# Attention and mixture-of-experts in one kernel: the attention's steps in a new order, token reads on half the array's rows, small work moved between engines

## The chip, the cores and the metric

The kernel runs on one core of a Trainium2 chip. The metric is the device time of one execution in microseconds (us). Before the change the median of 3 runs is 542.32 us (542.18 to 542.85).

## The reference

Two parts follow each other: an attention between tokens and a few states, and a mixture of experts over all their results.

```python
B, H, S, Ns, D = (8, 8, 512, 32, 64)
scores = scale * x @ state^T                 # (B, H, 512, 32)
a = softmax(scores)                          # over the 32 states
xread = a @ state                            # token reads, (B, H, 512, 64)
scores2 = scale * state @ x^T                # (B, H, 32, 512)
a2 = softmax(scores2)                        # over the 512 tokens
sread = a2 @ x                               # state reads, (B, H, 32, 64)
x = concat(xread, sread) -> (B, 544, 512)    # heads side by side
logits = x @ w_gate                          # 8 experts
local_gate = sigmoid(x @ w_local)
for b, s:                                    # in order of s
    e = argmax(logits[b, s]) if s == 0 or local_gate[b, s] < 0.5 else e of s - 1
    p = softmax(logits[b, s])
    out[b, s] = p[e] * (relu(x[b, s] @ w1[e]) @ w2[e])
```

The 8 expert layers are 512 to 1024 to 512 wide, and 8 x 544 = 4352 rows go through them. All data are float32.

## The kernel before

The kernel has three stages: attention, routing, experts. The scheduler is off: every engine executes its instructions in the order in which the program issues them.

**Attention** takes the batches one by one. The 8 heads of a batch are two groups u = 0 and 1 of four heads k; one PSUM tile s of 128 x 512 holds for one u the scores of 4 heads x 32 states against 512 tokens. The class Attention has one small method for each step, and the string STEPS gives the order: each word is a two-letter code and its indices, batch first, then the group u or a 128-token chunk c. So `tr20` is the turn of batch 2, group 0. What each step is, with its engine and its line of the profile:

| codes | engine, line | what it does |
|---|---|---|
| xt, xn | SP, L273, L277 | loads halves of a batch's transposed tokens x_t (512 KB each), its tokens x_n (1 MB) |
| sc | PE, L307 | scores, 16 matmuls on 64x32 tiles of the array |
| mx, nb | DVE L315, POOL L319 | maxima over tokens; times -scale |
| et, iv | ACT L323, DVE L328 and L329 | exponents over tokens with their sums; 1 over the sum |
| tu, ec | PE L377, ACT L381 | these exponents transposed; the copy to SBUF |
| sr, st, ws | PE L390, ACT L396, SP L405 | state reads; scaled; to DRAM |
| rt, sl, sk | DVE L400, PE L410, DVE L414 | state reads turned; the states' logits; their copy into lt |
| tr, mo, sb | DVE L334, DVE L337, POOL L344 | scores turned in 32x32 blocks; maxima over states; subtracted |
| ex, zh, zs, zi, ml, tb | ACT L348, POOL L355, DVE L358, DVE L363, POOL L367, DVE L371 | exponents; half sums; sums; reciprocals; products, called shares; turned back, as a |
| lg, lt | PE L422, DVE L426 | token logits from a; turned into the tile lt |
| vv, xr, wr | PE L432, ACT L438, SP L446 | token reads of a chunk; their copy to SBUF; to the DRAM tensor rows |
| ga, gl, sd | PE L289, ACT L294, ACT L268 | states times gate weights; kept as gl; states put into the blocks of a block-diagonal tile sd |
| ch, kp, wm, go | | choice of experts for batches 0 to 6; filler matmuls; hand over to the routing |

Token logits need no token reads: a times (states times gates) gives them. So the reads vv may come late, and about a third of them stand behind the first `go`. Two PSUM pools of four banks each serve the stage: sp for the scores, p for all other results of PE.

**Routing** (Routing.route) first makes the choice for batch 7 (`self.choose(lt, B - 1, B)`: six small DVE instructions on lt), then turns `top`, scans it along the tokens, turns it back, counts tokens by expert with two matmuls (`tot`, `pre`), and by some forty small DVE instructions finds each token's slot. At seven places it calls `reads()`, which issues the steps up to the next `go`. ACT has a few instructions in this chain: the exponent `pr` (L553), `less` (L607), `behind` (L612). Then matmuls of 0/1 matrices (L710) give the tokens of each slot, and GpSimd gathers the first rows (L827).

**Experts**: up to 24 pairs of 128-row blocks. The first pair is plain matmuls (L1100), the later ones use a seven-product scheme (L1016, L1056), with weights loaded by SP (L873) and sums on DVE (L930).

Of the kernel before, what the change touches and what calls it, by code (L numbers as in the profile page):

```python
# [8 lines left out]
F32 = mybir.dt.float32  # L9
# [3 lines left out]
Alu = mybir.AluOpType  # L13
AX = mybir.AxisListType.X
# [4 lines left out]
P = 128  # L19
B, H, S, N, DH = 8, 8, 512, 32, 64  # L20
D = H * DH
E, F = 8, 1024
T = S + N
# [127 lines left out]
sc0 kp3 xt11 xt10 mx00 ga kp2 sd3 tr01 xt21 mx01 sd2 mo01 nb0 tr00 et01 sb01 xn0 mo00 wm14 sc1 et00 sb00 ex01  # L151
iv0 tu01 tr11 gl tu00 zh01 ex00 tr10 xt20 ec00 zh00 zs01 mo10 sd0 xn1 zs00 sb10 zi0 ec01 mx11 sd1 sr0 ml01 mo11
ex10 mx10 sc2 ml00 st0 xt30 tb01 rt0 sb11 tb00 sl0 xt31 tr20 lg0 nb1 ex11 zh10 sk0 tr21 vv03 et10 zh11 xt41 zs10
vv00 et11 lt0 mx21 xr03 xt51 zs11 tu11 zi1 xr00 tu10 iv1 ml11 mo21 vv02 xt50 ec10 mo20 ml10 sc3 ec11 tb11 xt40
xr02 mx20 sb21 sr1 tb10 xn2 tr30 sb20 ex21 lg1 mx30 st1 vv12 zh21 ex20 rt1 tr31 nb2 sl1 zh20 et20 vv10 zs21 sk1
lt1 ws1 zs20 et21 tu20 zi2 xt60 mo30 xr10 ml20 sc4 xr12 iv2 mx31 ec20 xn3 ml21 tu21 tb20 vv11 mx41 ec21 nb3 sb30
et30 tb21 sr2 tr40 et31 xt61 lg2 mo31 ex30 tu30 mo40 sb31 st2 sc5 lt2 wr00 xr11 mx40 ec30 zh30 tr41 wr03 tu31
ex31 nb4 zs30 sb40 vv23 et40 mx50 xt70 ec31 mo41 tu40 zh31 ex40 rt2 sr3 sb41 zs31 ws0 xr23 zi3 xn5 et41 iv3 sl2
ml31 mx51 vv22 ex41 sk2 iv4 st3 ml30 tb31 sc6 xr22 rt3 ec40 zh41 tb30 xt71 sl3 zh40 zs41 lg3 tr50 nb5 vv31 wr02
zs40 et50 zi4 vv01 xn4 lt3 xr31 ml40 mo50 sk3 tr51 xr01 vv13 ml41 tb40 et51 vv21 mo51 sb50 xr13 wr10 iv5 vv20  # L160
tb41 xr21 sb51 xn6 mx60 ex50 lg4 mx61 xr20 zh50 tu50 ex51 lt4 tu41 tr60 nb6 ec50 zh51 tu51 zs50 et60 mo60 vv32
wr20 ec51 zs51 sb60 zi5 tu60 ec41 wr23 tr61 sc7 xr32 ml50 wr11 ex60 mo61 sr4 et61 ml51 tb50 wr12 mx71 sr5 sb61
ws2 st4 tb51 ec60 ws3 vv30 tr70 zh60 ex61 xn7 mx70 st5 lg5 zh61 xr30 zs60 tu61 mo70 nb7 et70 vv40 zs61 sb70 zi6
ec61 tu70 lt5 wr22 iv6 xr40 ml61 rt5 sr6 rt4 ex70 tr71 wr40 ec70 ml60 mo71 sl5 et71 wr13 sl4 sk5 tb61 vv41 sb71
st6 wr31 tb60 tu71 zh70 ex71 sk4 iv7 wr32 lg6 rt6 xr41 zs70 zh71 sl6 ec71 lt6 wr21 vv42 zs71 zi7 wr01 sr7 sk6
xr42 ml71 ch0 wr42 vv33 st7 ml70 wr41 vv50 tb71 xr33 wr33 tb70 vv53 xr50 rt7 wr30 lg7 xr53 sl7 lt7 wr53 vv51 sk7
go wr50 vv43 xr51 wr51 go xr43 vv52 wr43 vv61 xr52 ws4 vv60 wr52 xr61 go ws5 xr60 vv62 wr60 go xr62 ws7 wr62
vv71 wr61 vv72 xr71 wr71 vv63 xr72 wr72 vv70 xr63 go wr63 go xr70 wr70 ws6 go vv73 xr73 wr73
# [3 lines left out]
class Attention:  # L172


    def __init__(self, ctx, tc, p, late, xn, xt, st, stt, wgl, wgs, lt, rows, none):
# [14 lines left out]
        self.sttc = [once.tile([P, n, KT, N], F32, name=f"sttc{i}") for i, n in enumerate((1, B - 1))]  # L190
# [3 lines left out]
        self.states_of = once.tile([P, B * G * DH], F32, name="states_of")  # L194
        nc.sync.dma_start(out=self.states_of, in_=st)
        nc.sync.dma_start(out=self.sttc[1], in_=stt[:, 1:])
        nc.sync.dma_start(out=wgs.rearrange("p w k e -> p (w k e)"), in_=wgl)
# [3 lines left out]
        self.sd = late.tile([P, B, G * GD], F32, name="sd", bufs=1)  # L201
# [10 lines left out]
    def clear(self):  # L212
        nc = self.nc
        for z in self.zh:
            nc.vector.memset(z[:, :, N // 2:], 1e-9)
        for z in self.z2:
            nc.vector.memset(z[:, :, 1:], 1e-9)
        nc.gpsimd.memset(self.gl, 0.0)
        nc.gpsimd.memset(self.lt, 0.0)
        nc.gpsimd.memset(self.sd, 0.0)  # L220
        nc.gpsimd.memset(self.none, 0.0)
# [8 lines left out]
    def reads(self):  # L230
# [4 lines left out]
                  ec=self.turned_to, iv=self.invert, sr=self.state_reads, st=self.states_to, rt=self.states_turned,  # L235
                  ws=self.states_to_rows, sl=self.state_logits, sk=self.state_logits_kept, lg=self.logits,
                  lt=self.logits_turned, vv=self.token_reads, xr=self.reads_kept, wr=self.reads_to_rows,
                  sd=self.diagonal, ga=self.gates, gl=self.gates_kept, ch=self.choose, kp=self.keep, wm=self.warmed)
# [23 lines left out]
    def choose(self, i):  # L262
        self.route.choose(self.lt, 0, B - 1)

    def diagonal(self, k):
        r = slice(32 * k, 32 * k + 32)
        to = self.sd[r].rearrange("p b (g d) -> p b g d", g=G)
        self.nc.scalar.copy(to[:, :, :, DH * k:DH * k + DH],  # L268
                            self.states_of[r].rearrange("p (b g d) -> p b g d", b=B, g=G))

    def load_t(self, b, h):
        x = self.new(self.xp, f"x_t{h}", (b,), [P, KT // 2, S])
        self.nc.sync.dma_start(out=x.rearrange("p k s -> p (k s)"), in_=self.xt[b][:, h * D * 2:(h + 1) * D * 2])  # L273

# [4 lines left out]
    def states(self, b):  # L279
        return self.sttc[b > 0][:, b - (b > 0)]  # L280

    def gates(self):
        nc = self.nc
        self.ws = [self.bank() for u in range(G)]
        for u, w in enumerate(self.ws):
            r = slice(64 * u, 64 * u + 64)
            for b in range(B):
                for k in range(KT):
                    nc.tensor.matmul(w[32 * k:32 * k + 32, b * (E + 1):(b + 1) * (E + 1)],  # L289
                                     lhsT=self.states(b)[r, k, :], rhs=self.wh[r, k, :], start=True, stop=True)  # L290

    def gates_kept(self):
        for u, w in enumerate(self.ws):
            self.nc.scalar.copy(self.gl[:, :, u, :E + 1], w[:, :B * (E + 1)].rearrange("p (b e) -> p b e", b=B))  # L294
# [31 lines left out]
    def invert(self, b):  # L326
        i2 = self.get("i2", b)
        self.nc.vector.tensor_reduce(i2, self.z2[b % 4], axis=AX, op=Alu.add)  # L328
        self.nc.vector.reciprocal(i2, i2)  # L329
# [83 lines left out]
    def state_logits_kept(self, b):  # L413
        self.nc.vector.tensor_copy(self.lt[:N, b, SC, :E + 1], self.get("rl", b))  # L414

    def logits(self, b):

        l = self.of["l", b] = self.bank(n=P)
# [6 lines left out]
    def logits_turned(self, b):  # L425
        self.nc.vector.transpose(self.lt[:, b, :SC, :].rearrange("p i e -> p (i e)"), self.get("l", b))  # L426

    def token_reads(self, b, c):
        v = self.of["v", b, c] = self.bank()
        for u in range(G):  # L430
            d = slice(u * GD, u * GD + GD)
            self.nc.tensor.matmul(v[:, d], lhsT=self.get("a", b, u)[:, c * P:c * P + P], rhs=self.sd[:, b, d],  # L432
                                  start=True, stop=True)

    def reads_kept(self, b, c):
        xr = self.new(self.late, "xr", (b, c), [P, D], bufs=12)
        v = self.get("v", b, c)
        self.nc.scalar.copy(xr.rearrange("p (k u d) -> p u k d", k=KT, u=G),  # L438
                            v.rearrange("p (u k d) -> p u k d", u=G, k=KT))

    def reads_to_rows(self, b, c):
# [3 lines left out]
        t = b * T + c * P  # L445
# [793 lines left out]
```

## Time and profile before

| what | value |
|---|---|
| median of 3 runs | 542.32 us |
| profiled execution: its own time | 547.71 us |
| profiled execution: span | 545.9 us, mean granted PE clock 0.990 |
| busy share PE / DVE / ACT / POOL | 97% / 70% / 32% / 59% |
| DMA | 155.41 MB, mean 285 GB/s |
| first matmul of the first expert pair (L1100) | 97.27 us |

Busy shares are means over three stages with different limits, so each stage has to be read for itself. An instruction of DVE, ACT or POOL waits in its engine's queue, and all behind it wait too. In the lists of waits a row is: engine and line that waited, engine and line that released it, us in total, times, longest. In the groups a row is: line, engine, operation, output and inputs, shapes, count, then busy us and mean ns of one, then idle us before them and what ended it. In the busy times by stretch each engine has its busy us and, in brackets, its instructions; behind them stand the granted clock, the DMA share and GB/s.

### The profile page before, as it was taken

The page shows a single profiled execution, that of the slowest core. Times are in us where ns is not written, and L with a number is a line of the kernel's source. Part 1 is how long each engine was busy: PE and PEld are TensorE (multiplying, and loading weights), DVE is VectorE, ACT ScalarE, POOL GpSimd, SP SyncE. Part 2 cuts the span into 40 slices and gives each one's busy share as a digit, 9 for nine tenths or more (in the row PEclk, how much of TensorE's full clock was granted, in tenths as well). Part 3 has the DMA queues.
Part 4 walks back from the last instruction along what each step waited for, and adds up shares of the span by engine and source line. Part 5 has one row for each costly group of instructions (what it writes and reads, how often), then busy time and mean ns, then how long its engine had stood idle before and what let it go on. Part 6 is the DMA issues. An engine that isn't in the chain of part 4 may idle for free.

```text
span 545.9 us, 12958 instructions
## 1 busy us (share of the span) xinstructions
PE 527.0 (97%) x4913; PEld 460.0 (84%) x4916; DVE 381.0 (70%) x623; ACT 174.1 (32%) x359; POOL 319.4 (59%) x384
## 2 busy tenths in 40 slices
PE   8799888999999999999999999999999999999995
PEld 2566766988989898989898888889999999989994
DVE  6999877747665848575665848476777767677775
ACT  6698654112213222222213131313222322223221
POOL 7788702564584756565655555555756575746654
PEclk9899998999999999999999999999999999999998
DMA  8999776799989899897979798874657383856652
GB/s 318 393 325 372 258 255 232 247 394 395 405 281 360 332 318 384 294 379 272 381 284 372 288 361 295 340 243 142 215 219 280 113 315 117 291 150 239 210 217 100
DMA packets 48971, 155.41 MB, mean 285 GB/s; under 512 B 6849, under 2 KB 8001, under 8 KB 45570
## 3 DMA queue, kind: packets, MB, share of 16 engines
q1 hardware_dynamic: 41234, 135.78, 68.2%
q0 software_dynamic: 7520, 18.62, 9.5%
q8 instruction: 42, 0.69, 0.5%
q14 instruction: 31, 0.25, 0.1%
q10 hardware_dynamic: 144, 0.07, 0.1%
HBM read 136.61 MB, written 17.89 MB: 283 GB/s over the span
## 4 chain that ended last, share of the span: by engine, by line
PE 87%; DVE 7%; DMA 3%; issue 1%; POOL 1%; ACT 0%; DVEq 0%
PE ps L1056 23%; PE ps L1016 20%; PE sum L1016 15%; PE sum L1056 13%; PE ps L916 3%; PE ps L904 3%; PE ps L1100 3%; PE p L432 2%; DMA x_n<-in_xn_dram 2%; PE ps L710 2%; PE p L390 1%; DMA x_t<-in_xt_dram 1%; DVE a L371 1%; PE p L377 1%; PE p L422 1%
## 5 line engine op out<-in xcount | busy, mean ns | idle before, releaser
L821 POOL DMA_INDIRECT xg<-rows,row x131 | 156.4, 1194 | 30.3 <-issue 29.4
L930 DVE TENSOR_TENSOR a<-a,a 128x1024 f32<-128x1024 f32 x64 | 76.8, 1221 | 20.3 <-DMA a<-in_w_dram 18.9
L1016 PE MATMUL ps<-xt,a 128*128 128x128 f32 x720 | 89.2, 277 | 0.0
L1016 PE MATMUL sum<-xs,a 128*128 128x128 f32 x720 | 87.9, 275 | 0.0
L1016 PEld LDWEIGHTS ps<-xt,a 128*128 128x128 f32 x720 | 84.7, 192 | 2.3 <-issue 2.0
L1016 PEld LDWEIGHTS sum<-xs,a 128*128 128x128 f32 x720 | 84.0, 192 | 0.2 <-issue 0.2
L930 DVE TENSOR_TENSOR c<-c,c 128x1024 f32<-128x1024 f32 x64 | 75.4, 1220 | 3.3 <-DMA c<-in_w_dram 2.6
L1056 PE MATMUL ps<-c,h 128*128 128x256 f32 x312 | 74.7, 382 | 0.0
L1056 PEld LDWEIGHTS ps<-c,h 128*128 128x128 f32 x312 | 58.0, 190 | 10.9 <-issue 3.7
L1056 PE MATMUL ps<-c,hs 128*128 128x256 f32 x256 | 60.5, 379 | 0.0
L1056 PEld LDWEIGHTS ps<-c,hs 128*128 128x128 f32 x256 | 48.6, 190 | 6.6
L996 POOL DMA_INDIRECT out_dram<-y,tok x32 | 37.4, 1170 | 26.2 <-DVE y L1083 13.8
L1056 PE MATMUL sum<-c,h 128*128 128x256 f32 x200 | 47.2, 379 | 0.0
L835 POOL COPY tick<-r 1x1 f32<-1x1 f32 x41 | 21.1, 514 | 42.1 <-ACT r L1061 39.6
L930 DVE TENSOR_TENSOR h<-s,s 128x512 f32<-128x512 f32 x15 | 10.4, 692 | 49.6 <-issue 27.6
L1056 PEld LDWEIGHTS sum<-c,h 128*128 128x128 f32 x200 | 38.0, 190 | 5.2
L835 POOL COPY tick<-s 1x1 f32<-1x1 f32 x45 | 15.7, 349 | 43.2 <-ACT s L1039 43.1
L964 ACT COPY sum<-ps 128x256 f32<-128x256 f32 (+1 forms) x31 | 14.3, 460 | 74.9 <-PE ps L1016 53.4
L849 DVE STREAM_TRANSPOSE xt<-xg 128x512 f32<-128x512 f32 x32 | 33.5, 1082 | 1.1 <-DMA xg<-rows,row 1.1
L432 PE MATMUL p<-sd,a 128*128 128x256 f32 x128 | 32.1, 390 | 0.0
L1061 ACT ACTIVATE r<-sum,prob 128x256 f32<-128x256 f32 x32 | 15.1, 473 | 52.0 <-PE sum L1056 35.2
L1056 PE MATMUL sum<-c,hs 128*128 128x256 f32 x128 | 30.2, 379 | 0.0
(230 smaller groups left out, 759.6 us busy)
## 6 DMA issues: line engine op xcount, KB each, us to landing
a<-in_w_dram SPq DMA_DIRECT2D x68, 512.0 KB
c<-in_w_dram SPq DMA_DIRECT2D x68, 512.0 KB
at<-in_w_dram SPq DMA_DIRECT2D x18, 1024.0 KB
ct<-in_w_dram SPq DMA_DIRECT2D x18, 1024.0 KB
x_t<-in_xt_dram SPq DMA_DIRECT2D x16, 512.0 KB
x_n<-in_xn_dram SPq DMA_DIRECT2D x8, 1024.0 KB
rows<-xr SPq DMA_DIRECT2D x32, 256.0 KB
xg<-rows,row POOLq DMA_INDIRECT x131
```

The lines of the kernel that those rows point to most:

```text
L432: self.nc.tensor.matmul(v[:, d], lhsT=self.get("a", b, u)[:, c * P:c * P + P], rhs=self.sd[:, b, d], start=True, stop=True)
L821: nc.gpsimd.indirect_dma_start(out=to.rearrange("p x k -> p (x k)"), out_offset=None, in_=rows.rearrange("n q x -> (n q) x"), in_offset=ba ...
L835: nc.gpsimd.tensor_copy(tick, value)
L849: nc.vector.transpose(to.rearrange("p k (i t) -> p k i t", i=Q), xgs_[u % 2][:, b].rearrange("p i x k -> p k i x"))
L904: nc.tensor.matmul(hps[SQ * g:SQ * g + SQ, :], lhsT=self.x_t[:, j, :], rhs=a[:, j, :, g], start=(j == 0), stop=(j == KT - 1))
L916: nc.tensor.matmul(yps[SQ * g:SQ * g + SQ, :], lhsT=self.h[:, m, :], rhs=ct_[:, 2 * m // FK, g // 2, m % (FK // 2), g % 2 * P:g % 2 * P + ...
L930: nc.vector.tensor_tensor(out, a, b, op=op)
L996: put = nc.gpsimd.indirect_dma_start(out=out, out_offset=to, in_=y, in_offset=None, bounds_check=NT - 1, oob_is_err=False)
L1016: nc.tensor.matmul(to[:, m * P:m * P + P], lhsT=w[:, j, m * P:m * P + P], rhs=x[:, j, :], start=begin and m == 0 and j == 0, stop=(m == FK ...
L1056: nc.tensor.matmul(to, lhsT=x[:, m, :], rhs=w[:, m, :], start=begin and m == 0, stop=(m == FK // 2 - 1), skip_group_check=True)
L1061: nc.scalar.activation(to, t, Act.Copy, scale=p)
L1100: nc.tensor.matmul(hps[:, i * P:i * P + P], lhsT=a[n][j // 2][:, j % 2, i * P:i * P + P], rhs=x_t[:, j, b * P:b * P + P], start=(j == 0), ...
```

## The change

- STEPS is another order of nearly the same steps. Batches are taken as 0, 1, 2, 3, 6, 5, 4, 7 instead of 0 to 7. The first `go` now has 14 of the 32 copies of token reads ahead of it instead of 21.
- Token reads: the step `vv` now takes two chunks and both halves of the array's rows. A half (64 rows) holds two heads, and its moving operand is a batch's states padded with zeros to 128 columns, loaded from DRAM as such (1 MB, step `lc`). The four copies into sd (`sd`) and its memset on GpSimd are gone. `xr` copies one half; `wr` writes two chunks (512 KB); the copies have four buffers of 512 KB instead of twelve of 256 KB.
- The states' logits `sk` are copied by ACT instead of DVE. The sum of `iv` becomes a step `ia` on GpSimd. For batches 0 to 5 the token logits come out of PE with tokens on partitions (a as the stationary operand, 9 columns), and ACT copies them into lt; batches 6 and 7 stay as they were.
- The gates `ga`, `gl` are done for one group u at a time. The states' loads are split: batch 1 alone (`la`), batches 2 to 7 and the gate weights (`lb`), the padded states (`lc`).
- The choice for batches 0 to 6 is five steps `ca` to `ce` instead of one.

```diff
 STEPS = """
-sc0 kp3 xt11 xt10 mx00 ga kp2 sd3 tr01 xt21 mx01 sd2 mo01 nb0 tr00 et01 sb01 xn0 mo00 wm14 sc1 et00 sb00 ex01
-iv0 tu01 tr11 gl tu00 zh01 ex00 tr10 xt20 ec00 zh00 zs01 mo10 sd0 xn1 zs00 sb10 zi0 ec01 mx11 sd1 sr0 ml01 mo11
...
-xr42 ml71 ch0 wr42 vv33 st7 ml70 wr41 vv50 tb71 xr33 wr33 tb70 vv53 xr50 rt7 wr30 lg7 xr53 sl7 lt7 wr53 vv51 sk7
-go wr50 vv43 xr51 wr51 go xr43 vv52 wr43 vv61 xr52 ws4 vv60 wr52 xr61 go ws5 xr60 vv62 wr60 go xr62 ws7 wr62
-vv71 wr61 vv72 xr71 wr71 vv63 xr72 wr72 vv70 xr63 go wr63 go xr70 wr70 ws6 go vv73 xr73 wr73
+lb xt10 sc0 kp3 la xt11 mx00 xt21 tr01 ga0 mo01 xn0 tr00 sb01 mo00 sc1 gl0 mx01 sb00 ex01 ga1 tr10 zh01 ex00
+xt20 mx10 nb0 zh00 et00 zs01 mo10 xn2 gl1 tu00 et01 zs00 sb10 zi0 tr11 ec00 tu01 ia0 ex10 mo11 ml01 sc2 ec01 iv0
+mx11 xn1 sb11 sr0 tb01 ml00 mx20 ex11 mx21 st0 zh11 tr20 xt31 nb1 mo20 nb2 et11 zh10 rt0 zs11 sb20 et10 xt30 kp6
...
+ec71 zs71 lg4 zi7 sk4 sk5 iv7 ml70 wr11 sr7 ml71 tb70 lt4 ca vv40 st7 tb71 ws7 rt7 lg7 cb xr400 cc sl7 xr401 lt7
+sk7 cd vv70 wr40 ce go vv61 xr701 xr700 go wr70 vv41 xr611 xr610 xr410 vv71 wr61 xr411 go xr710 wr41 vv51 xr711
+vv60 wr71 xr510 xr511 go xr601 vv50 wr51 xr600 vv30 xr501 wr60 xr500 xr300 vv31 wr50 xr301 go go wr30 xr311
+xr310 wr31 go
 """
...
-        self.sttc = [once.tile([P, n, KT, N], F32, name=f"sttc{i}") for i, n in enumerate((1, B - 1))]
+        self.sttc = [once.tile([P, n, KT, N], F32, name=f"sttc{i}") for i, n in enumerate((1, 1, B - 2))]
...
-        self.sd = late.tile([P, B, G * GD], F32, name="sd", bufs=1)
+        self.sd = late.tile([P, B, G, 2, DH], F32, name="sd", bufs=1)
...
-        nc.gpsimd.memset(self.sd, 0.0)
...
+    def load_second(self):
+        self.nc.sync.dma_start(out=self.sttc[1], in_=self.inputs[0][:, 1:2])
+
+    def load_states(self):
+        self.nc.sync.dma_start(out=self.sd.rearrange("p b u k d -> p (b u k d)"), in_=self.inputs[1])
+
+    def load_others(self):
+        stt, st, wgs, wgl = self.inputs
+        self.nc.sync.dma_start(out=self.sttc[2], in_=stt[:, 2:])
+        self.nc.sync.dma_start(out=wgs.rearrange("p w k e -> p (w k e)"), in_=wgl)
...
     def invert(self, b):
-        i2 = self.get("i2", b)
-        self.nc.vector.tensor_reduce(i2, self.z2[b % 4], axis=AX, op=Alu.add)
-        self.nc.vector.reciprocal(i2, i2)
+        self.nc.vector.reciprocal(self.get("i2", b), self.get("i2", b))
+
+    def totals(self, b):
+        self.nc.gpsimd.tensor_scalar(self.get("i2", b), self.z2[b % 4][:, :, 0], 1e-9, None, Alu.add)
...
     def state_logits_kept(self, b):
-        self.nc.vector.tensor_copy(self.lt[:N, b, SC, :E + 1], self.get("rl", b))
+        self.nc.scalar.copy(self.lt[:N, b, SC, :E + 1], self.get("rl", b))
 
     def logits(self, b):
 
+        if b < 6:
+            l = self.of["l", b] = self.bank(n=SC * (E + 1)).rearrange("p (i e) -> p i e", i=SC)
+            for i in range(SC):
+                for u in range(G):
+                    self.nc.tensor.matmul(l[:, i], lhsT=self.get("a", b, u)[:, i * P:i * P + P],
+                                          rhs=self.gl[:, b, u, :E + 1], start=(u == 0), stop=(u == G - 1))
+            return
...
     def logits_turned(self, b):
+        if b < 6:
+            self.nc.scalar.copy(self.lt[:, b, :SC, :E + 1], self.get("l", b))
+            return
...
-    def token_reads(self, b, c):
-        v = self.of["v", b, c] = self.bank()
-        for u in range(G):
-            d = slice(u * GD, u * GD + GD)
-            self.nc.tensor.matmul(v[:, d], lhsT=self.get("a", b, u)[:, c * P:c * P + P], rhs=self.sd[:, b, d],
-                                  start=True, stop=True)
+    def token_reads(self, b, j):
+
+        v = self.of["v", b, j] = [self.bank().rearrange("p (c k u d) -> p c k u d", c=2, k=2, u=G) for h in range(2)]
+        for c in range(2):
+            t = slice((2 * j + c) * P, (2 * j + c) * P + P)
+            for u in range(G):
+                for h in range(2):
+                    r = slice(64 * h, 64 * h + 64)
+                    self.nc.tensor.matmul(v[h][:, c, :, u, :], lhsT=self.get("a", b, u)[r, t], rhs=self.sd[r, b, u],
+                                          start=True, stop=True)
...
-        xr = self.new(self.late, "xr", (b, c), [P, D], bufs=12)
...
+        xr = self.new(self.late, "xr", (b, j), [P, 2, 2, D // 2], bufs=4)
...
-        nc.vector.tensor_reduce(self.mx[:, c].rearrange("p c o -> p (c o)"), lf[:, :, :E], axis=AX, op=Alu.max)
...
+        def largest():
+            nc.vector.memset(lt[0:1, b0:b1, 0, E:E + 1], -1.0)
+            nc.vector.tensor_reduce(self.mx[:, c].rearrange("p c o -> p (c o)"), lf[:, :, :E], axis=AX, op=Alu.max)
...
+        return largest, less, numbers, first, gated
```

## The prediction

> **What bounds the kernel now.** I read the list of granted clocks first (0.990 over the span: nothing disturbed), then the page's shares and chain, then busy times by stretch, then the waits of each engine inside the stretch that the change edits. One execution was profiled: its span is 545.9 us, its own time 547.71 us. The runs shown have a median of 542.32 us, 5.4 us less. Savings below are taken from the span and then put on the median.
>
> By stretch (us; busy PE, PE loads, DVE, ACT, POOL, then clock and DMA):
>
> ```profile
> 8.10:72.05 63.95, 57.02 (x1107) 40.22 (x1107) 57.45 (x141) 48.20 (x108) 45.62 (x56) 0.97 0.91 341
> 72.05:97.27 25.22, 22.10 (x167) 16.06 (x168) 18.15 (x58) 13.21 (x31) 2.96 (x3) 0.93 0.66 231
> 97.27:545.90 448.63, 441.49 (x3616) 402.02 (x3616) 301.16 (x408) 109.12 (x210) 264.12 (x312) 1.00 0.77 280
> ```
>
> The first row runs from the first maximum on VectorE to the end of the choice for batch 7, a moment that I call E (72.05 us); the second is the routing, up to the first expert matmul; the third is the experts, where TensorE is 98% busy. The change edits the first row and the reads scattered in the second. If E comes earlier, the rest follows by as much unless something in it is late.
>
> In the first row PE and DVE look alike, so I ask who waited. VectorE's waits there:
>
> ```profile
> DVE lt L414 <- PE p L410: 1.6, 1, 1.6
> DVE e L334 <- PE s L307: 1.0, 1, 1.0
> DVE rt L400 <- ACT ys L396: 1.0, 1, 1.0
> DVE lt L426 <- PE p L422: 1.0, 1, 1.0
> DVE a L371 <- POOL e L367: 0.3, 1, 0.3
> DVE nb L315 <- PE s L307: 0.3, 1, 0.3
> ```
>
> VectorE is busy 57.45 of 63.95 us; 5.2 of its 6.5 idle us are these waits. It is the bound of the stretch. GpSimd's waits show that it is next:
>
> ```profile
> POOL e L344 <- DVE m L337: 4.0, 6, 1.2
> POOL nb L319 <- DVE nb L315: 2.7, 1, 2.7
> POOL e L367 <- DVE i L328: 2.7, 1, 2.7
> POOL e L367 <- DVE lt L521: 2.4, 1, 2.4
> POOL e L367 <- DVE z L363: 2.1, 2, 1.1
> ```
>
> Every one is for VectorE. From 10.09 to 67.15 us (first to last instruction of attention) GpSimd is busy 45.6 of 57.1 us, idle 11.45. The groups that the change moves:
>
> ```profile
> L426 DVE STREAM_TRANSPOSE lt<-p 128x128 f32<-128x128 f32 x8 | 2.3, 291 | 1.1 <-PE p L422 1.0
> L414 DVE COPY lt<-p 32x9 f32<-32x9 f32 x8 | 1.0, 130 | 1.6 <-PE p L410 1.6
> L328 DVE TENSOR_REDUCE i<-z 128x2 f32<-128x4 f32 x8 | 1.0, 125 | 0.1
> L432 PE MATMUL p<-sd,a 128*128 128x256 f32 x128 | 32.1, 390 | 0.0
> L438 ACT COPY xr<-p 128x512 f32<-128x512 f32 x32 | 18.6, 585 | 11.1 <-PE p L432 10.2 <-ACT others L634 0.9
> ```
>
> **What the Trainium skill says.** "TensorEngine Tiling (Array Packing)", Tiling Modes: tiles of the array work independently, a change of mode drains it. The trace agrees on the first: the scores (L307, 64x32 tiles) take 1.02 us for 16 matmuls of 512 columns, where full-array 256-column matmuls (L1056) take 0.216 us each (8 in 1.73 us of the chain). No run here prices the drain. Same page, Restrictions and Gotchas: row tiles write to different PSUM banks; the new reads take two banks each, untested so far. "TensorE: Matmul & The Clock Gate", Part 1: an idle array falls to half clock. The trace agrees: idle from 14.31 us, clock 0.50 from about 16.8 to 20. "GPSIMD Engine Reference", Key points: GpSimd shares SBUF interfaces with VectorE and can't read PSUM; the work moved to it is in SBUF, and the price below is one measured beside a busy VectorE.
>
> **The change, part by part.**
>
> *Off VectorE.* Eight L328 at 125 ns, eight L414 at 130 and six of eight L426 at 291: 3.8 us. The rows of this stretch sum to 64.7 us for 57.45 us of busy time (instructions overlap at their ends), a factor of 0.89, so 3.4 us of path. VectorE then needs 54.05 us.
>
> *Its four big waits.* Start: the first maximum stays at 8.10 us, since batch 0's x_t is still first in SP's queue. L334's 1.0 us (12.3 us) was for batch 1's scores, behind 0.5 MB of states in SP's queue; these 0.5 MB (now 1 MB) move behind the first thirteen x_t loads, and at the 410 GB/s of those microseconds that is 1.2 us. L400's 1.0 us was for batch 0's state read, waiting for x_n; scores of batch 2 now stand ahead of it and several VectorE operations ahead of rt0. L414's 1.6 us is ScalarE's now. L426's 1.0 us at the end is covered by two slices of the choice (0.99 and 1.22 us) between the last turn back and lt7. So 4.6 us go; 1.9 us (two small waits and 1.3 of issue) stay. That gives E = 8.10 + 54.05 + 1.9 = 64.05 us if GpSimd keeps up.
>
> *GpSimd.* It gets eight sums, priced as its like L319 (218 ns): 1.7 us. Its attention work is 16 x (1.048 + 1.062 + 0.735) + 16 x 0.218 = 49.0 us; by the overlap seen (45.6 busy for 46.7 in the rows) 47.8. It can start when VectorE has done three operations, at 9.9 us, and end at 57.7 plus its idle time i. After its last product VectorE still has tb71, rt7, four slices of the choice, lt7 and the choice for batch 7: 0.65 + 0.27 + 0.99 + 1.22 + 0.47 + 0.14 + 0.3 + 1.12 = 5.2 us. So **E = 62.9 + i**. Each new sum waits for ScalarE's second exponent over tokens, with a subtraction or product queued behind it, then VectorE's turn back. Bounds for i: 0 and today's 11.45. With VectorE 3.4 us lighter and its stalls gone its results come sooner, so I take 3.5, about a third: E = 66.4, **5.65 us earlier**.
>
> *ScalarE* loses four L268 (4.2 us), gains eight L414 and six L426 as copies (nearest row: the gates' copy, 228 ns; 3.2 us), and in this stretch has 14 copies of reads instead of 21 (7 x 0.585 = 4.1 us). From 48.2 it falls to about 43 us: hidden. If that cover went, each copy of logits waiting on PE would hold an exponent behind it.
>
> *TensorE.* 128 reads of 256 columns at 0.216 us (27.6 us) become 128 of 128 columns on half the rows: 0.112 us each without overlap (L1016's 16 in 1.79 us), 0.056 in pairs, so 14.3 or 7.2 us. Six batches' logits go from 0.65 us to 8 x 0.112 = 0.9. All hidden behind VectorE: counted as nothing, and that is also the answer if tiles don't pair. What it costs if the cover goes is the clock rival below.
>
> *Queues.* SP: 32 writes of 256 KB become 16 of 512 KB, the same bytes. Up to batch 7's last x_t SP's order has 16.3 MB; 0.7 MB had moved by 5 us in the trace of before, so at 410 GB/s it lands about 5 + 15.6 / 0.41 = 43 us. It is also behind two writes that need copies at about 39; and VectorE needs it at about 48 (44.6 us of its rows lie ahead: 8.1 + 44.6 x 0.89), so hidden. GpSimd loses the 3.5 us memset, before its first subtraction: hidden by the wait for scores.
>
> *Routing.* Before E 14 copies of reads are done, 18 remain (11 before). Sixteen stand ahead of ScalarE's `less`, 14 of them after the exponent `pr`, which ends about E + 1.0. Back to back at the 0.49 us that two L381 copies show, `less` comes at E + 7.9; without overlap (0.585) E + 9.2. Before it was E + 8.5, including 1.5 us in which transposes stood behind long reads on PE; that goes, but `tot` now waits behind vv60, whose bank needs the eighth copy: E + 4.8 to 5.1 against 4.9. The copies' buffers, twelve of 256 KB before, are four of 512 KB: a write moves in 1.28 us at 410 GB/s, a pair of copies is made in 1.0, so the buffer of xr30 comes free near E + 7.1, just as it is wanted. I take 0, with -0.9 and +1.5 as ends. The experts' code is the same: 0, within 0.3.
>
> **Sum.** 545.9 - 5.65 = 540.25 us of span, 542.06 for that execution; on the median 542.32 - 5.65 = **536.7 us**.
>
> **Rivals.** *Forecast* (0.55): i between 2 and 6 us, E 64.9 to 68.9, time 535.2 to 539.2. Another 0.10 for i under 2, where VectorE's own floor, E = 64.05, gives 534.3, and the routing's lower end 533.4.
>
> *Array at half clock* (0.20). The reads kept PE at 38.6 of 40 us between 20 and 60; without most of them its work is about 43 us of 58 (scores 8.4, state reads 8.4, turns 7, logits 6.4, state logits 2.6, gates 1.3, fillers 3, eight of the sixteen reads 4 to 7). At half clock each batch's scores are 1.05 us later; if VectorE can't cover half of that, 8 x 0.5 = 4 us come off the gain: 540.7. For it: the half clock at 16.8 us. Against: a gap of 1.8 us at 59.2 left the clock at 1.00, and six fillers stand in the new order.
>
> *GpSimd becomes the bound* (0.15), the case that ends slower. With the sums it has 47.8 us of work for a stretch that is now 57 us long and is to shrink, and each sum adds a wait on ScalarE in its one queue. If its idle time stays at 11.45, E is 74.35: 544.6. It decides from i = 9.15 us. For it: 4.0 us of its idle time is for L337, which stays on VectorE. Against: the waits at L328 and L521 (5.1 us) go with the work that caused them.
>
> **How the numbers follow.** Likeliest 536.7. A difference within 0.2% (1.1 us) can't be told from none. Faster by more: nearly all of 0.55 + 0.10 + 0.20, less the clock's worst: 0.82. No change 0.05, slower 0.13. The range 533.5 to 541.6 leaves out some 0.03 below and 0.16 above.
>
> **What would show it.** Right: E near 66 with VectorE 54 us busy in its stretch; no VectorE wait for L414's or L426's successors over 0.5 us; GpSimd idle 2 to 6 us; token reads near 7 us of PE; `less` at E + 8. Wrong: GpSimd idle over 9 us, a clock of 0.50 for over 10 us between 20 and 60, or E early and the first expert matmul not.

## The result, and the profile after

The changed kernel takes 551.26 us (median of 6 runs, 548.96 to 552.9) against 542.83 for the kernel before on the same chip. The ratio estimated from these runs is 1.0125, with a 95% interval of 1.0101 to 1.0149; the quotient of the two medians is higher, 1.0155, so the loss is told here as 6.8 to 8.4 us. The forecast was 536.7, a gain; the change makes the kernel slower.

The profiled execution after has a span of 548.6 us (own time 550.4), only 2.7 us over the one before. The profile before was of a long execution: its expert pairs, in code that the change leaves alone, take 29.04 us each (first matmuls of L904, start to start) and those after 28.74. So the two are compared up to the experts. E, the end of the choice for batch 7, moved from 72.05 to **75.23 us**; the first expert matmul from 97.27 to 101.69. By stretch, cut as before (us; busy PE, PE loads, DVE, ACT, POOL, then clock, DMA share and GB/s):

```profile
7.68:75.23 67.55, 60.38 (x1158) 47.09 (x1159) 54.28 (x119) 42.31 (x111) 47.28 (x64) 0.85 0.84 307
75.23:101.69 26.46, 22.85 (x248) 17.21 (x247) 18.12 (x58) 15.88 (x38) 2.97 (x3) 0.86 0.82 285
101.69:548.60 446.91, 440.04 (x3619) 402.10 (x3616) 302.38 (x408) 109.42 (x210) 259.19 (x312) 0.99 0.79 281
```

PE is TensorE. VectorE is busy 54.28 us, 3.2 less than before, in a stretch 3.6 us longer: 13.3 us idle instead of 6.5. PE did not get lighter: 60.38 us instead of 57.02, at a clock of 0.85 instead of 0.97. Whom VectorE waits for (us in total, times, longest):

```profile
DVE nb L315 <- PE s L307: 6.2, 5, 2.5
DVE rt L401 <- ACT ys L397: 3.2, 2, 2.9
DVE mx L537 <- PE p L423: 2.0, 1, 2.0
DVE a L372 <- POOL e L368: 1.5, 2, 1.2
DVE lt L437 <- PE p L430: 1.3, 1, 1.3
```

The four waits of before were 4.6 us; now PE's results alone cost 9.5 us (L315, L537, L437), and the 3.2 us at L401 are a state read of PE, scaled by ScalarE, that came late. GpSimd from its first to its last attention instruction (9.80 to 67.80 us):

```profile
POOL e L345 <- DVE m L338: 8.4, 6, 6.0
POOL e L368 <- DVE i L327: 2.7, 1, 2.7
...
POOL i L330 <- ACT e L323: 0.9, 1, 0.9
```

It is busy 47.3 us and idle 10.7. The longest wait of the first row, 6.0 us, ends at 9.80 and lies ahead of this stretch; what is left of the waits for VectorE is 7.7 us, and the new sums (L330) wait 0.9 us. What PE does more of is in the groups. The weight loads (PEld) stand beside the matmuls; the last line is the logits' row of the kernel before:

```profile
L447 PE MATMUL p<-sd,a 64*128 64x128 f32 x256 | 20.7, 302 | 1.0 <-DMA sd<-in_st_dram 0.5 <-ACT xr L452 0.5
L423 PE MATMUL p<-gl,a 128*128 128x9 f32 x96 | 11.6, 257 | 0.0
L423 PEld LDWEIGHTS p<-gl,a 128*128 128x128 f32 x96 | 11.2, 192 | 1.9 <-ACT lt L435 0.8 <-ACT xr L452 0.8
L422 PE MATMUL p<-a,gl 128*32 128x128 f32 x128 | 5.4, 277 | 1.2 <-DVE a L371 1.0 <-PE p L390 0.2
```

Six batches' logits in the new form are 11.6 us, 1.93 each; in the old form eight were 5.4 us, 0.68 each. The reads fell from 32.1 to 20.7 us, not to 7.

In the routing, `less`, an instruction of ScalarE for which VectorE's chain has to wait, comes at 85.53, 10.3 us after E instead of 8.5; ScalarE's copies of reads (L452) wait there for writes to give their buffers back:

```profile
ACT xr L452 <- DMA rows<-xr: 1.5, 3, 1.1
```

### The profile page after: what moved, and what is told of

Same layout as the page of the kernel before. It is cut to its first block, busy times and chain, and to the rows that moved or that the text cites. A ratio compares the mean times of both kernels' runs of the same rounds, so it can differ in the third digit from the quotient of the medians.

```text
span 548.6 us, 13185 instructions
## 1 busy us (share of the span) xinstructions
PE 529.5 (97%) x5041; PEld 468.0 (85%) x5044; DVE 376.4 (69%) x601; ACT 171.2 (31%) x369; POOL 312.6 (57%) x391
## 4 chain that ended last, share of the span: by engine, by line
PE 89%; DMA 7%; DVE 2%; issue 0%; ACT 0%; SPq 0%; ACTq 0%; DVEq 0%
PE ps L1082 23%; PE ps L1042 20%; PE sum L1042 15%; PE sum L1082 13%; PE ps L942 3%; PE ps L930 3%; DMA x_t<-in_xt_dram 3%; PE ps L1126 3%; PE p L447 3%; PE ps L736 2%; PE p L391 2%; DMA x_n<-in_xn_dram 2%; DMA sd<-in_st_dram 1%; PE p L423 1%; DMA rows<-xr 1%; PE s L307 1%
## 5 line engine op out<-in xcount | busy, mean ns | idle before, releaser
L847 POOL DMA_INDIRECT xg<-rows,row x131 | 158.9, 1213 | 33.6 <-issue 32.6
L956 DVE TENSOR_TENSOR a<-a,a 128x1024 f32<-128x1024 f32 x64 | 76.8, 1222 | 29.8 <-DMA a<-in_w_dram 28.4
L861 POOL COPY tick<-r 1x1 f32<-1x1 f32 x41 | 16.5, 403 | 40.9 <-ACT r L1087 38.2
L990 ACT COPY sum<-ps 128x256 f32<-128x256 f32 (+1 forms) x31 | 14.3, 460 | 71.0 <-PE ps L1042 49.5
L875 DVE STREAM_TRANSPOSE xt<-xg 128x512 f32<-128x512 f32 x32 | 33.5, 1082 | 0.8 <-DMA xg<-rows,row 0.8
L1042 PE MATMUL ps<-xs,a 128*128 128x128 f32 x240 | 29.2, 275 | 0.0
```

The lines of the kernel that those rows point to most:

```text
L847: nc.gpsimd.indirect_dma_start(out=to.rearrange("p x k -> p (x k)"), out_offset=None, in_=rows.rearrange("n q x -> (n q) x"), in_offset=ba ...
L861: nc.gpsimd.tensor_copy(tick, value)
L875: nc.vector.transpose(to.rearrange("p k (i t) -> p k i t", i=Q), xgs_[u % 2][:, b].rearrange("p i x k -> p k i x"))
L956: nc.vector.tensor_tensor(out, a, b, op=op)
L1042: nc.tensor.matmul(to[:, m * P:m * P + P], lhsT=w[:, j, m * P:m * P + P], rhs=x[:, j, :], start=begin and m == 0 and j == 0, stop=(m == FK ...
```

## The experiments

Ratios are estimated in the same way, to the kernel before run beside; brackets hold the 95% interval, and one per cent is 5.4 us. Where two variants are compared by their ratios, they may have run on different chips, each beside the kernel before. E and `less` are from the one profiled execution of each.

| label | ratio | E, us | `less` after E, us | first expert matmul, us |
|---|---|---|---|---|
| before (first profile) | 1 | 72.05 | 8.5 | 97.27 |
| after | 1.0125 [1.0101, 1.0149] | 75.23 | 10.3 | 101.69 |
| old_logits | 1.0026 [1.0003, 1.0048] | 71.8 | 10.3 | 97.89 |
| more_buffers | 1.0128 [1.0055, 1.0201] | 79.7 | 9.2 | 105.23 |
| early_xn | 1.0109 [1.0073, 1.0146] | 74.5 | 10.0 | 100.64 |
| before_logits | 1.0133 [1.0098, 1.0167] | 77.0 | 8.6 | 102.32 |
| loads | 0.9978 [0.9961, 0.9994] | 67.86 | 10.3 | 94.10 |
| loads_bufs | 0.9962 [0.9947, 0.9977] | 67.61 | 9.0 | 92.95 |
| before_small | 1.0055 [1.0035, 1.0074] | 73.3 | 8.4 | 98.97 |
| before_apart | 1.0029 [1.0016, 1.0042] | 72.6 | 8.6 | 98.11 |
| best_vec | 0.9926 [0.9898, 0.9954] | 67.18 | 8.9 | 92.20 |
| logits_3 | 1.0011 [0.9998, 1.0023] | 70.6 | 8.9 | 95.62 |
| best_2 | 0.9937 [0.9915, 0.9959] | 66.8 | 9.1 | 92.04 |
| old_reads | 1.0196 [1.0156, 1.0236] | 76.5 | 13.8 | 107.02 |
| old_reads_2 | 1.0102 [1.0079, 1.0125] | 72.3 | 13.8 | 102.83 |
| old_reads_3 | 1.0137 [1.0109, 1.0165] | 74.5 | 13.8 | 105.03 |

### The new form of logits

old_logits undoes it in the changed kernel, before_logits does it alone in the kernel before (its copy on ScalarE), logits_3 puts it for three batches into the best kernel found.

```diff
-        if b < 6:
+        if b < 0:      # old_logits, in logits and logits_turned
+        if b < 3:      # logits_3
```

> The changed kernel with one part undone: all eight batches' token logits in the old form (32 columns of gates stationary, 128 tokens moving, a VectorE transpose into lt), not only batches 6 and 7. In the changed kernel one batch's logits in the new form take 1.9 us of TensorE (16 records; old form 0.6), and the clock falls to 0.50 just after them (28.9 and 70.3 us). Theory 'logits': this form is most of the loss, TensorE being full from 17 to 58 us, so undoing it takes 3 to 7 us off the changed kernel's 551: 544 to 548. Rival 'late tokens' (batch 5's x_n lands at 60.7 us and everything behind it waits): 0 to 1 us, 550 to 551. Rival 'VectorE': 6 transposes of 0.29 us come back to VectorE, so it is 1.5 us slower.

> The kernel before with only the logits of batches 0 to 5 in the new form (a stationary, 9 columns moving, copied into lt by ScalarE), everything else as it was. Theory 'logits': 6 x 1.3 us more on a TensorE that is 97% full from 20 to 60 us, against 6 x 0.29 us less on VectorE: 3 to 7 us slower than before, 546 to 550, and more so if the clock falls as well. Rivals 'late tokens' and 'VectorE': 0 to 1.5 us faster, 541 to 543.

> The best_vec kernel (0.9926 of before: old logits, loads ahead, six buffers, small moves undone) with the new form of logits for batches 0 to 2 alone, copied by ScalarE. Six batches of it cost the changed kernel 1.0 % (1.0126 against 1.0026). Theory 'time of TensorE': each batch takes 1.25 us more of TensorE and the loss is in proportion, 2 to 3.5 us, ratio 0.996 to 0.999. Rival 'clock or threshold' (the loss comes only when TensorE is full or its clock falls, which six batches bring and three do not): under 1 us, 0.992 to 0.9945.

Undone, 1.0 % of the time comes back (1.0125 to 1.0026). Alone, in the old order, it costs as much as the whole change did (1.0133, 7.2 us, just over the 3 to 7 written), and E goes to 77.0. Three batches of it cost 0.85 % (0.9926 to 1.0011), some 4.6 us, by intervals that allow 2.4 to 6.8; the two profiled executions differ by 3.4 us (543.12 and 539.69). That fits a cost of PE's time, and the rival's "under 1 us" is out: three batches are enough. It does not show that the clock has no part in logits_3, where it is 0.50 from 26 to 32 us, against 26 to 28 in best_vec. In before_logits PE is busy 64.62 of 68.90 us up to E at a clock of 0.95, close to before's 0.97: the loss there is PE's time, not its clock.

Why it costs so much is in the weight loads. The kernel before in the old form, by groups, and below it another group of the same kernel, the states' logits:

```profile
L422 PEld LDWEIGHTS p<-a,gl 128*32 128x32 f32 x128 | 3.2, 109 | 2.8 <-ACT xr L438 1.5 <-issue 0.7 <-ACT e L348 0.3
L410 PE MATMUL p<-wgs,rt 128*32 128x9 f32 x64 | 3.2, 178 | 1.8 <-issue 1.8
```

The old form keeps 32 columns of gates in the array and moves 128 columns of a past them; the new one keeps 128 columns of a and moves 9 of gates. A load of 32 columns is 3.2 / 128 = 0.025 us, one of 128 columns 11.2 / 96 = 0.117 us, and the new matmuls take 11.6 / 96 = 0.121 us each. The states' logits (L410) also move nine columns, past 32 loaded ones, and take 3.2 / 64 = 0.050 us. The Trainium skill, "TensorE: Matmul & The Clock Gate", LDWEIGHTS (loading the stationary operand), has it so: the price of a load goes by its columns P, about P / 1.2 ns, which gives as an estimate 107 ns for 128 columns and 27 for 32. The trace agrees, with 117 and 25. Nine moving columns save nothing when 128 have to be loaded for them.

### Late loads

early_xn gives x_n four buffers and puts two of its loads earlier in the changed kernel. loads does the same on old_logits, and moves three more:

```diff
-        x = self.new(self.xp, "x_n", (b,), [P, SC, G, KT, DH])
+        x = self.new(self.xp, "x_n", (b,), [P, SC, G, KT, DH], bufs=4)
 STEPS (loads)
-mo01 xn0 tr00 ... ex00 xt20 mx10 ... tb20 ws1 sb31 ... sr2 xt51 tb21 ... mx60 lc zh31
+mo01 xt20 xn0 tr00 ... ex00 mx10 ... tb20 xt51 lc ws1 sb31 ... sr2 tb21 ... mx60 zh31
 STEPS (both)
-xn4 nb4 ... sr6 st3 ... ws6 xr000 sl3 mx70 xn5 ... lg5 xn7 mo71
+xn4 xn5 nb4 ... sr6 xn7 st3 ... ws6 xr000 sl3 mx70 ... lg5 mo71
 STEPS (best_2, on best_vec)
-mo10 xn2 gl1 ... et10 xt30 kp6
+mo10 gl1 ... et10 xt30 xn2 kp6
```

> The changed kernel with four instead of three buffers for x_n, and the loads of batch 5 and 7 placed directly behind batch 4's and behind batch 6's state read, ahead of the states' row writes that SP waited 2 to 4 us for. Theory 'late tokens': batch 5's x_n lands near 54 us instead of 60.7, the TensorE gap at 58.5 to 60.9 and the half clock from 60.5 to 66.5 go: 3 to 5 us faster than the changed kernel, 546 to 548. Rival 'logits': TensorE is full either way, under 1.5 us: 549.5 or more.

> The changed kernel with the old form of logits for all batches, and its loads ahead: batch 2's x_t half before x_n of batch 0, batch 5's second half and the padded states before the first write of state reads, four buffers for x_n, x_n of batches 5 and 7 earlier. With the old logits alone it was 1.0026 of before; there TensorE waited 4.3 us for x_t (1.54 for batch 2 at 17.1 us, 2.75 for batch 5 at 38.6 us) and 2.9 us for x_n of batch 5 at 61 us, and VectorE waited 6.1 us for scores and 2.0 us for state reads. Theory 'late loads' (the rest of the forecast gain is lost to transfers that stand behind a waiting write in SP's queue): these waits go, the choice of batch 7 ends 3 to 5 us earlier, at 67 to 69 us, ratio 0.993 to 0.997. Rival 'the order' (VectorE waits because TensorE's steps stand in that order, whatever the loads do, or because the DMA rings are full up to 38 us and an earlier load only makes another one late): the waits come back under other names, the end stays within 1 us of 71.8, ratio 1.001 to 1.004.

In the changed kernel the earlier x_n brought nothing that can be told (1.0109 against 1.0125). With PE lighter, these edits bring 0.5 % (1.0026 to 0.9978), and E comes to 67.86. PE's waits in old_logits,

```profile
PE s L307 <- DMA x_t<-in_xt_dram: 4.3, 2, 2.8
...
PE p L391 <- DMA x_n<-in_xn_dram: 2.9, 1, 2.9
```

became, in loads,

```profile
...
PE s L307 <- DMA x_t<-in_xt_dram: 3.0, 2, 2.1
...
PE p L447 <- DMA sd<-in_st_dram: 1.5, 1, 1.5
PE p L391 <- DMA x_n<-in_xn_dram: 0.8, 1, 0.8
```

and VectorE's wait for scores went from 6.1 to 3.5 us. The longest wait of old_logits was made by SP's queue: the second half of batch 5's x_t was issued at 31.46 us, behind a write of state reads at which SP stood from 26.84 to 30.73. The theory held for 2.6 of the 3 to 5 us that it gave, and its rival held in part: the waits for x_t at 17 and 38.6 us are gone, but two new ones stand at 25 us (2.15 us) and at 30.6 (0.86). The longest row of PE's list in loads, 3.3 us at state reads (2.5 of them at 58.4 us), names no releaser, so its cause stays open.

> As best_vec, with the tokens x_n of batch 2 loaded behind batch 3's x_t halves instead of ahead of batch 1's x_n. TensorE waits 1.9 us for x_t at one place there, and x_n of batch 2 is not read until about 30 us. Theory 'a megabyte in the wrong place': that wait goes and VectorE gains 0.5 to 1.5 us, ratio 0.990 to 0.992. Rival 'covered': VectorE does not wait for these scores, within 0.5 us of best_vec, 0.9915 to 0.9935.

Moving a megabyte of x_n behind two more x_t loads took the wait for x_t away and changed nothing (0.9937 against 0.9926): covered.

### Buffers of the writes

```diff
-        xr = self.new(self.late, "xr", (b, j), [P, 2, 2, D // 2], bufs=4)
+        xr = self.new(self.late, "xr", (b, j), [P, 2, 2, D // 2], bufs=6)
```

> The changed kernel with six buffers of 512 KB for the copies of token reads instead of four. Theory 'write buffers': in the routing ScalarE's copies waited 1.5 us for row writes to free a buffer and `less` stood behind them, VectorE lost 1.23 us there; with six the loss goes: 1.2 us faster than the changed kernel, about 550. Rival: the writes are bound by DMA and the wait moves to the next copies or to the index's copy: 0, 551.

> As loads, and six buffers instead of four for the copies of token reads. In the old-logits kernel ScalarE's copies in the routing waited for buffers that the writes held, and `less` came 10.3 us after the choice in the changed kernel, where the forecast had 7.9 to 9.2. Theory 'write buffers': `less` comes 1 us earlier, the time is 0.5 to 1.2 us below loads. Rival: the copies wait for TensorE's reads or ScalarE's own time, the difference to loads is under 0.5 us either way.

In both, `less` comes about 1.2 us sooner after E (10.3 to 9.2; 10.3 to 9.0). In the changed kernel no gain shows in an interval 1.5 % wide; on loads it is 0.16 %, 0.9 us, with intervals that overlap. The profiled E of more_buffers is 4.5 us later than that of after with the same order of steps: one profile of such a kernel is not its median.

### The small moves off VectorE

before_small makes two of them in the old order, before_apart the same with time between sum and reciprocal, and best_vec undoes them in loads_bufs.

```diff
-        self.nc.vector.tensor_copy(self.lt[:N, b, SC, :E + 1], self.get("rl", b))
+        self.nc.scalar.copy(self.lt[:N, b, SC, :E + 1], self.get("rl", b))
...
-        self.nc.vector.tensor_reduce(i2, self.z2[b % 4], axis=AX, op=Alu.add)
+        self.nc.gpsimd.tensor_scalar(i2, self.z2[b % 4][:, :, 0], 1e-9, None, Alu.add)
         self.nc.vector.reciprocal(i2, i2)    # before_apart: three VectorE steps later
```

> The kernel before with only two moves off VectorE: the states' logits copied by ScalarE, the sums of the exponents over tokens by GpSimd. That takes 8 x (125 + 130) ns = 2.0 us of rows off VectorE, by the 0.89 of the forecast 1.8 us of path. Theory 'VectorE binds the old order': 1 to 2 us faster, ratio 0.996 to 0.998, the choice of batch 7 at 70 to 71 us instead of 72. Rival 'coupled engines' (VectorE's idle time grows by what its work shrinks, since GpSimd, ScalarE and TensorE hold it in turn): within 0.5 us of before, ratio 0.999 to 1.001.

> As before_small, but the sums on GpSimd stand right behind the second exponent over tokens and the reciprocals at least three VectorE instructions later, so that nothing waits for a sum just ordered. Theory 'handoff' (before_small lost because VectorE stood at each reciprocal for 0.9 us, 6.2 us in all): these waits fall under 1.5 us, and the 1.8 us of path come out: ratio 0.995 to 0.999. Rival 'coupled engines' (in the old order TensorE, VectorE and GpSimd hold each other in turn, and lighter VectorE work is only idle time): VectorE's waits go to other names, ratio 1.000 to 1.004.

> As loads_bufs (0.9962 of before), with the two small moves undone: the states' logits are copied by VectorE again and the sums of the exponents over tokens are VectorE's. In loads_bufs VectorE waited only 0.2 us for those sums on GpSimd; in the old order it waited 6.2 us for them (before_small, 1.0055). Theory 'the moves pay where the order keeps the sum and its reciprocal apart': VectorE gets 16 instructions of 125 and 130 ns back, 1.8 us of path, 1 to 2 us slower than loads_bufs, ratio 0.998 to 1.000. Rival 'VectorE has idle time now' (6 to 8 us in its stretch): within 0.5 us of loads_bufs, 0.995 to 0.997.

Neither theory of before_small held: it is slower. Its waits, in one line of VectorE's list:

```profile
DVE i L329 <- POOL i L328: 6.2, 7, 1.5
```

Eight sums of 125 ns left VectorE, and it stood 6.2 us for the results. Held apart, that wait is gone, but the kernel is still 0.3 % slower than before, as 'coupled engines' had it, and waits for GpSimd stand elsewhere: 2.4 us for products (L374), 1.6 us for half sums (L361), while GpSimd's new sums wait 3.5 us for ScalarE. In the new order, where the sums are apart too, undoing the moves costs nothing: 0.9926 against 0.9962, intervals that overlap a little. VectorE up to E, in loads_bufs and then in best_vec (us; busy PE, PE loads, DVE, ACT, POOL, clock, DMA):

```profile
7.90:67.61 59.71, 46.80 (x1158) 32.77 (x1158) 55.06 (x125) 40.77 (x105) 47.13 (x64) 1.00 0.90 345
```

```profile
7.90:67.18 59.28, 49.11 (x1159) 34.88 (x1158) 56.19 (x141) 40.25 (x97) 45.35 (x56) 0.94 0.91 348
```

1.1 us more of VectorE's work, and E 0.4 us earlier: VectorE had the time. Of the 1.8 us by which best_vec then reaches its first seven-product pair (112.61 against 114.42), 1.05 are its first expert matmuls, 3.84 us instead of 4.89 for the same 32 at another clock (1.00 from 92 to 96 us, against 0.50 and 0.69); so the gain over loads_bufs is not shown to come from the moves.

### The token reads

Three kernels go back to the old form of reads (128 rows, 256 columns, the block-diagonal tile with its memset and four copies): old_reads on old_logits, old_reads_2 and old_reads_3 on loads with the copies at other places.

```diff
-                    self.nc.tensor.matmul(v[h][:, c, :, u, :], lhsT=self.get("a", b, u)[r, t], rhs=self.sd[r, b, u],
+                self.nc.tensor.matmul(v[c][:, d], lhsT=self.get("a", b, u)[:, t], rhs=self.sd[:, b, d],
                                       start=True, stop=True)
 STEPS (lc, the states' load, stands ahead of ws1 in old_reads, behind xt31 in the others)
+et60 sd0 ... sk1 sd1 ... ex61 sd2 ... ec60 sd3    (old_reads)
+lg0 sd0 ... ec10 sd1 ... et21 sd2 ... ec11 sd3    (old_reads_2)
+et31 sd0 ... ex31 sd1 ... ex30 sd2 ... et60 sd3   (old_reads_3)
```

> The changed kernel with the old form of logits and the old form of token reads too (full rows, 256 columns against a block-diagonal tile, with its memset and four copies on ScalarE, and the states' load of 0.5 MB ahead of the first write of state reads): what is left of the change is the order, the two small moves off VectorE and the split loads. TensorE gets about 8 us more work ahead of the first `go` (32 records of 0.39 us a piece less 0.06 times as many columns), ScalarE 4.2 us. Theory 'the order needs the light reads' (TensorE at 51 of 64 us in the old-logits kernel was near its limit): 2 to 5 us slower than the old-logits kernel, ratio 1.006 to 1.012. Rival (reads are hidden in any form, as the forecast had it): within 1 us of it, ratio 1.001 to 1.005.

> The loads kernel (0.9978 of before) with the old form of token reads alone: full rows, 256 columns, block-diagonal states, with the memset and four copies on ScalarE, the copies now spread over 24 to 29 us so that no read waits for them, and the states' 0.5 MB loaded behind batch 3's first x_t half. In old_reads 3.9 us of TensorE's time went to waiting for these copies. Theory 'the light reads are worth time' (eight reads of two chunks ahead of the first go at about 2.0 us of TensorE instead of 1.0 to 1.2, and longer blocks ahead of scores and turns): 2.5 to 5 us slower than loads, ratio 1.002 to 1.007. Rival 'hidden', as the forecast had it: within 1 us of loads, 0.996 to 1.000.

> As old_reads_2 (loads with the old form of token reads; 1.0102), with the four copies of the states some 5 us later on ScalarE, at 31 to 35 us, when the states are there: in old_reads_2 the first copy held ScalarE for 2.4 us, with an exponent behind it. Theory 'the light reads are worth time in two places' (eight reads ahead of the first go, and the eight to nine behind it, on which `less` waits: 13.9 us after the choice there against 10.4 in loads): still 3 to 6 us slower than loads, ratio 1.003 to 1.009, `less` 12.5 to 14 us after the choice. Rival 'only the copies' wait': back to within 1.5 us of loads, 0.997 to 1.001, `less` at 10 to 11.

The old form costs 1.7 % on old_logits (9.2 us) and 1.2 to 1.6 % on loads (6.7 to 8.6 us), more than the expectations gave. Part of it is certain: `less` stands 13.8 us behind E in all three and 10.3 in loads, so 3.5 us are lost in the routing, where no copy of states is left. From E to `less` ScalarE's copies of reads wait there for PE's reads, in old_reads_2

```profile
ACT xr L458 <- PE p L453: 5.2, 8, 1.8
```

against 2.4 us, two times, in loads, and PE is busy all of these 13.8 us. The part ahead of E (4.5 us in old_reads_2, 6.7 in old_reads_3) moves with the place of the four copies, 4.2 us of ScalarE; how much of it is PE's is not settled. Putting the copies later, as old_reads_3 did, did not help.

### The kernel before, once more

> The kernel before, unchanged, for a second profile: the first was of an execution of 547.71 us, 5 us over the median. If the difference lay in the expert pairs (29.05 us each there against 28.73 in the profile after), as the comparison of the two traces says, then a typical execution has the choice of batch 7 at 71 to 72.5 us as before and pairs of 28.6 to 28.8 us; if it lay in attention, the choice ends at 67 to 70 us.

The one execution took 548.33 us, again over the median of 544.45. E is at 72.42, close to the first profile's 72.05; but the first 32 expert matmuls take 6.14 us instead of 3.84, and its first seven-product pair starts at 121.36 instead of 117.71 (123.32 after). The pairs are then 28.7 us, as expected of a typical execution. So the first profile was long in its pairs, the second at its entry into the experts. No median execution of before has a profile. Of the 6.8 to 8.4 us of loss the first profile and that after show 5.6 by the first seven-product pair: 3.2 at E, 1.2 in the routing, and 1.2 in the first 32 expert matmuls (5.04 us instead of 3.84), which vary by more than that in the kernel before itself. Where the rest lies is left open.

The old order with the new reads alone wasn't tried.

## Why the prediction was wrong

**VectorE's work: right.** 54.05 us were worked out, 54.28 measured; ScalarE 43 against 42.3, GpSimd 47.8 against 47.3. The moves did what they say.

**TensorE "counted as nothing": the step that failed.** "Six batches' logits go from 0.65 us to 8 x 0.112 = 0.9" multiplied the calls in the code by a duration of the trace. The 0.112 us is from "16 in 1.79 us", and in the trace every float32 matmul of the code is two records: L422 has x128 for eight batches of 8 calls, L432 x128 for 64 calls. So 16 x 0.112 = 1.8 us was to be had from the same row, and 1.93 was measured: 1.25 us more a batch, 7.5 for six, and by old_logits 5.4 us of time. The reads had the same slip: "128 of 128 columns" are x256, and 14.3 or 7.2 us should have read 28.7 or 14.3; measured 20.7. At clock 1.00 sixteen records take 1.16 us, 0.073 each, nearer to the 0.056 of pairs than to 0.112; at clock 0.50 they take 2.08. PE's 43 us of the clock rival became 60.4. Over the whole attention logits are 13.3 us instead of 6.4, and scores, state reads and the turned exponents (L378) are 33.5 instead of 23.8; these three were 29.8 in the profile of before already.

In the prediction's sum E = 62.9 + i the loss sits in two terms: i, GpSimd's idle time, was 10.7 us instead of 3.5, and what follows its last product 7.4 instead of 5.2, since VectorE stood for PE.

**The cover was named, and not priced.** "All hidden behind VectorE" did not hold: VectorE's waits for PE rose from 3.9 to 9.5 us. The old_reads runs show the other side: PE's lighter reads are worth 3.5 us in the routing alone, which the forecast had at nothing.

**The four waits.** "So 4.6 us go": L334's and L414's went. L426's successor waits 1.3 us and the choice 2.0 more for batch logits (L537); L400's went from 1.0 to 3.2 us behind a late state read.

**SP's queue was followed for one tile only.** Batch 7's x_t was checked and was in time. Batch 2's x_t half (1.6 us in after), batch 5's half and its x_n were not, nor the write of state reads that two of them stand behind; loads shows what these places are worth, 2.6 us.

**GpSimd as the bound: the right side for the wrong cause.** Its idle time, 10.7 us, is over the 9.15 from which that rival decides, and 544.6 is the rival nearest to the result. That is luck: its mechanism, sums that wait for ScalarE, is 0.9 us in after, and GpSimd was idle mostly because VectorE was. In the old order the sums did cost, the other way round: in before_small VectorE waits 6.2 us for them.

**The clock rival: it happened in part, and not by its own cause.** By stretches of 2 us, PE is at half clock for 5.8 us between 20 and 60, under the 10 us that were named as the sign; up to E the mean clock is 0.85. One fall, to 0.50 from 60 to 66 us, comes behind 2.3 us in which PE waited for batch 5's x_n. But at 29 us the clock falls with no idle PE just before it. PE's timeline of after (start, us, what):

```profile
24.21 1.85 PE L423 MATMUL p<-gl,a 128*128 128x9 f32 x16
25.99 1.09 PE L307 MATMUL s<-x_t,sttc 64*32 64x512 f32 x16
27.01 1.95 PE L423 MATMUL p<-gl,a 128*128 128x9 f32 x16
```

and its stretches (busy columns as above, then clock):

```profile
26.00:28.00 2.00, 2.00 (x26) 1.16 (x25) 1.51 (x5) 1.10 (x3) 1.26 (x2) 1.00 0.17 66
28.00:30.00 2.00, 2.00 (x61) 1.98 (x64) 1.97 (x5) 0.99 (x4) 1.00 (x3) 0.80 0.87 193
30.00:32.00 2.00, 2.00 (x31) 1.83 (x24) 1.97 (x4) 0.85 (x4) 2.00 (x3) 0.50 1.00 393
```

PE is busy in every microsecond of this. The matmuls of nine columns stand ahead of the fall, but that they cause it is not shown: groups of them at 35 and 45 us in after have no fall behind them, and of six in before_logits only the first has (0.50 from 24 to 26 us, then 1.00 from 28 to 80). The Trainium skill, "TensorE: Matmul & The Clock Gate", Part 1, explains half clock by an idle array, which these lines don't show. The cause of this fall stays open.

**Routing "0, with -0.9 and +1.5 as ends".** Measured +1.24, inside; the step "the buffer of xr30 comes free ... just as it is wanted" failed, by 1.5 us of waits for buffers, and `less` came at E + 10.3 instead of 7.9 to 9.2. Six buffers bring it to about E + 9.

**How far the mechanism was right.** With the logits as before, the loads ahead, six buffers and the small moves undone, E comes at 67.2 us, where 66.4 was forecast, and the kernel takes 0.9926 of before, a gain of 4.0 us where 5.65 was forecast (best_vec, 539.8 us, the fastest here beside best_2). That is near the forecast, but not by its sum: VectorE is busy 56.2 us there instead of 54.05 and idle 3.1 instead of 4.3. The new order and the light reads carry that gain together; the order with the old reads is slower than before (1.0102 in old_reads_2), and the share of each is not shown. The logits on PE cost more than all of it, and no gain from the small moves is shown.

## What to carry to other kernels

Before a duration from a group is multiplied, count that group's records against the calls in the code, and price a matmul by the columns it loads as well as by those it moves. Work moved off the busiest engine has to be bought by another that has a gap at that very place: a moved instruction of 125 ns cost a wait of up to 1.5 us where its result was wanted at once. When a change shortens one engine's work, follow every load in the queue to its reader, not just the last one.

## What the runs showed of the hardware

- Two slices of the choice, 128x280 on VectorE with two inputs from SBUF each, took 0.96 and 1.18 us before, beside two products of GpSimd (64.89 to 67.15 us), and 0.41 and 0.45 after, when GpSimd had ended. Before:

```profile
65.29 0.96 DVE L523 TENSOR_TENSOR eq<-lt,mx 128x280 f32<-128x280 f32 x1
66.28 1.18 DVE L524 SCALAR_TENSOR_TENSOR eq<-eq,up 128x280 f32<-128x280 f32 x1
```

and after:

```profile
71.10 0.41 DVE L540 TENSOR_TENSOR eq<-lt,mx 128x280 f32<-128x280 f32 x1
71.54 0.45 DVE L543 SCALAR_TENSOR_TENSOR eq<-eq,up 128x280 f32<-128x280 f32 x1
```

  The Trainium skill, "GPSIMD Engine Reference", Key points, which the prediction cited for the shared SBUF interfaces, names instructions of VectorE with two SBUF inputs as those that contend with GpSimd; the trace fits, at over a factor of two on these.
- The first 32 expert matmuls took 3.84 or 6.14 us in two executions of one kernel (before and before_again); the granted clock was 1.00 from 98 to 100 us in the one and 0.50 from 98 to 102 in the other.
- The granted clock fell to 0.50 at 29 us in after, with PE shown busy in all of the 3 us before.
